# Attention with memory plus a gated feed-forward block on one core: w_v loaded first in two halves, a first layer norm in smaller tasks, and a new issue order

## The chip, the core and the metric

The kernel runs on one core of a Trainium2 chip. The core has a matrix engine (TensorE, PE in the profile; PEld is its loading of weights), a vector engine (VectorE, DVE), an engine for activation functions (ScalarE, ACT), a general engine (GpSimd, POOL) and SyncE (SP), which here only issues DMA transfers. ACT issues a few transfers of its own at the start. Engines run their own instruction streams in order and wait for each other by semaphores. The metric is device time in microseconds (us), the median of several runs.

## The reference

x is 2048 x 512 in bf16. It is normalised by rows, and both branches work on the result xn; x, A and B are added at the end.

```python
xn = _layernorm(x, axis=-1)
return x + _A_ref(xn, wq, wk, wv, wo, beta) + _B_ref(xn, w1, w2)
```

Branch A is attention in 32 heads of 16, over 4 segments of 512 rows one after the other. Within a segment it is causal softmax attention. Besides, a memory M (16 x 16 for each head) and a vector z run over the segments:

```python
pq = phi(qs)                       # phi(t) = t + 1 where t > 0, else exp(t)
a_mem = (pq @ M) / (pq . z + 1e-6)
o = g * a_mem + (1 - g) * a_dot    # g = sigmoid(beta), one for each head
M = M + phi(ks)^T @ vs;  z = z + sum(phi(ks))
```

The heads' outputs go through wo (512 x 512). Branch B is silu(xn @ w1) @ w2, with 1792 columns in between.

## The kernel before

All weights and one or two segments of activations stay in SBUF. The work is cut into some 1700 tasks, each one engine's short run of instructions, made by functions that add a task with its dependencies and buffers (`A(...)`, line 192). The tasks are issued in one fixed global order, the list `ORDER` of task numbers at line 64, which `Sched.run` (line 217) walks. On each engine the instructions stand in the order in which the list names its tasks. So an engine's order, and the buffer that a task gets from a ring, are settled when the program is built; the costs and due times in the task calls do not move anything once `ORDER` is written out. SP's DMA queue is in order as well: a transfer that waits for its data holds up every later one.

The main loop has 72 blocks of scores ("quads", line 899 and after), 18 for each segment. A block is: 4 to 12 matmuls of k (kB) and q (qT) for four head groups at a time, into psS, which takes four PSUM banks and exists once; an exp of all of it on ACT (L870, 128 x 2048 elements); and two causal masks on POOL (L889). The next block can begin when this exp has ended. Between two blocks TensorE does other matmuls, some ten of 512 columns: the projections to q, k and v, the feed-forward h (w_1) and its second product (w_2), the output projection (wo), the memory's products (M, psN), or one P times V (PV, two banks at once). These all share four other PSUM banks (`banks`), each of which must be copied out, mostly by DVE (the copies at L742, L790, L807, L958, L1178, L1203, L1228), before its next use.

Names used below: xn is a normalised tile of 128 rows (DVE, L617), xnT its transpose, stats the bn_stats of a tile (L583) with its aggregate (L584) and the addition of eps (L586), rstd the power -0.5 on POOL (L606). kB is k with every second head group masked out (L747 on POOL, for the first tile L721 and L723). V is the v projection with a column of ones; VS is V with its 64-row halves exchanged, made by two DMAs for each segment (L819). N and O are the copies of even and odd P times V; Z, Zg, Zr, dR and R are the steps by which the softmax denominators go through DRAM, are inverted, and come back repeated for every element of a head (den, Dr likewise for the memory's denominators); L1144 multiplies N by R. phiK is the transposed phi(k), made by a transposing DMA (L761).

The start, which the change touches: x's first four tiles are loaded one by one, two on SP's queue and two on ACT's; then half of w_k (its first 256 columns) on SP, half of w_q on ACT, then on SP all of w_v, w_1 in two halves with x's next four tiles between them, and the other halves of w_k and w_q. The first segment's layer norm (`ln(0)`) goes tile by tile. Tile 2 has its statistics from ACT (mean, sq), the other three from DVE, each in one task (stats, aggregate, eps). Then POOL's rstd, DVE's xn, four transposes on TensorE (L630) and one copy to xnT for each tile, on ACT for tiles 0 to 2 and on DVE for tile 3. TensorE meanwhile repeats a dummy matmul of the identity ("warm"). The first q and k tile is cut by row tiles; both, and v's first row tile, precede the first block of scores.

Of the kernel before, what the change touches and what calls it, by code (L numbers as in the profile page):

```python
# [10 lines left out]
BF16 = mybir.dt.bfloat16  # L11
# [53 lines left out]
1 3 5 14 27 0 2 53 63 28 29 15 30 31 32 64 33 54 34 4 35 36 58 55 37 38 39 40 41 42 65 59 60  # L65
43 44 45 66 70 46 71 47 56 57 48 49 50 51 67 61 62 72 52 96 109 16 6 110 68 69 97 111 7 8 9
10 98 73 74 18 114 115 99 17 116 11 112 113 100 117 19 147 101 102 184 118 103 136 129 12 130
185 131 187 148 149 132 137 150 104 105 138 188 189 268 269 270 139 76 75 271 272 13 151 133
280 106 281 282 283 140 77 284 78 84 124 273 186 192 125 107 285 126 127 193 143 81 128 274
275 82 276 277 119 120 121 122 21 123 135 196 168 278 279 169 170 108 83 171 194 172 286 287  # L70
288 289 163 164 197 142 141 190 200 79 298 299 300 301 292 80 293 290 294 85 295 291 134 86
199 201 302 87 165 89 166 167 204 152 153 154 296 297 155 328 198 329 330 202 331 205 156 179
303 203 90 180 173 332 333 88 208 209 181 191 195 182 159 144 145 304 158 305 157 160 183 220
222 221 210 212 213 306 307 161 352 353 354 355 356 214 215 358 308 309 382 383 384 385 216
217 310 311 312 386 206 313 314 363 364 146 315 428 429 430 357 431 175 226 227 211 365 366
367 432 316 317 318 319 207 218 320 22 321 371 372 373 374 230 671 219 672 673 674 223 231
375 228 176 234 177 433 225 368 235 675 229 434 224 91 435 436 420 437 174 421 390 391 178
376 392 393 237 92 238 239 322 323 324 325 326 422 394 443 444 445 236 446 377 676 423 424
241 242 243 438 439 327 440 369 447 441 20 240 359 334 335 336 337 442 338 339 677 678 246
247 401 402 403 404 405 232 340 360 341 342 343 346 347 348 349 93 450 23 233 250 679 361 244  # L80
680 344 345 350 351 94 245 409 410 411 412 413 251 248 370 262 264 254 487 252 488 406 407
489 572 162 451 452 453 454 455 456 457 458 459 460 461 462 463 464 465 466 397 255 256 253
580 490 263 467 491 258 259 257 492 362 681 493 494 517 689 690 691 692 693 495 249 496 571
587 588 398 497 498 260 499 261 579 581 682 518 519 694 500 425 501 520 399 400 582 589 387
521 583 522 523 524 388 590 591 265 266 449 469 584 448 683 592 684 685 573 686 687 525 389
595 526 527 596 267 695 696 697 24 698 502 574 426 427 585 528 529 530 531 599 688 503 594
504 593 505 597 701 702 703 704 506 408 470 471 699 700 395 577 578 507 600 602 705 508 603
872 873 874 586 601 509 875 510 511 512 532 706 604 533 416 534 598 606 535 607 536 605 513
608 514 515 623 417 475 610 611 537 476 538 516 713 25 575 576 378 472 539 624 26 540 714 715
379 380 719 716 541 477 612 615 720 396 721 717 718 625 478 722 542 543 876 544 616 545 755  # L90
756 757 479 619 758 836 837 838 546 839 483 614 723 724 759 831 731 481 613 732 609 733 734
618 620 629 832 735 833 707 474 415 840 708 736 841 842 617 621 418 853 834 835 473 709 710
843 844 482 630 711 622 633 846 712 847 848 634 468 845 849 850 626 627 637 414 638 381 812
813 814 815 743 766 744 628 635 480 767 768 769 641 485 762 486 484 553 554 555 877 816 559
556 745 560 631 878 746 561 642 562 645 640 770 557 774 636 737 775 738 776 760 739 777 747
748 740 547 643 563 548 646 879 649 564 778 632 549 550 741 742 644 817 1097 1098 647 1099
1100 650 551 565 566 567 648 1101 639 568 653 654 569 1102 95 665 419 771 761 804 805 806 667
807 781 763 881 880 764 808 725 882 779 657 658 998 666 656 1103 1104 1105 1106 1107 885 793
794 795 796 797 726 782 727 854 660 728 729 855 659 1108 652 661 662 655 1006 651 823 663 824
825 826 997 999 749 750 751 752 664 856 857 858 827 859 860 861 862 863 1013 864 865 730 785  # L100
786 787 788 866 867 753 754 798 868 869 1014 789 1127 1000 1128 870 1129 1130 1131 1017 765
1015 668 1005 913 914 1001 1002 780 669 887 772 1003 1004 915 852 1132 1007 1008 773 670 1018
1020 916 790 1011 917 888 1021 1012 1022 958 959 918 919 920 799 1024 960 921 922 923 961
1009 892 962 783 1025 800 801 1019 1133 924 925 1026 926 927 1010 1134 1135 1136 1137 963 964
1138 965 1029 1115 1116 1117 802 570 1118 1030 1109 1110 1111 1112 889 966 1113 851 1119 803
967 886 968 1114 1033 969 970 971 972 1016 1181 1023 1182 1031 1183 1196 1197 1198 894 1120
1199 1200 1034 1037 883 1188 1189 1190 1191 1032 1038 1192 1184 784 1028 1027 871 895 1185
# [1305 lines left out]
```

## Time and profile before

| what | value |
|---|---|
| median of 6 runs | 226.58 us (225.02 to 227.29) |
| the profiled execution's own time | 225.02 us |
| its span, first to last instruction | 223.3 us |
| granted TensorE clock | 1.00 |
| TensorE matmuls | 2800, busy 217.0 us |
| first and last block of scores begin | 11.38 and 200.94 us |
| DMA queues | SP 20.14 MB, ACT 0.52 MB |

The profile is one execution. Time in the text is counted from the span's start. A row such as "32.20 0.40 PE L504 MATMUL psS<-qT,kB" is an instruction, or a row of equal ones: start, length, engine, line of the kernel, operation, what it writes and reads; "[0.81 <-DVE N L958]" at its end says that its engine stood idle for 0.81 us before it, and whose end released it. All matmuls but transposes have line 504, that of a helper, so the names of their operands tell them apart: "ps<-xnT,w" is h, "ps<-w,hT" the second product of the feed-forward block, "ps<-Pt,V" and "ps<-Pt,VS" are P times V. Matmuls overlap (a matmul's length is longer than the distance to the next), so their price is read from start to start.

### The profile page before, as it was taken

How to read it: one execution, taken by the hardware profiler on the slowest of the kernel's cores; microseconds unless marked ns; L12 is line 12 of the kernel's file. 1: busy time of each engine (PE TensorE's matmuls, PEld its weight loads, DVE VectorE, ACT ScalarE, POOL GpSimd, SP SyncE). 2: the span in 40 equal slices, each digit the busy share in tenths (PEclk: the TensorE clock that was granted, in tenths of full speed). 3: DMA queues.
4: the chain of work that ended last, by engine and by line, in shares of the span. 5: the costliest groups of instructions: out<-in, count | busy, mean ns of one | idle time of the engine just before them, and what ended most of it. 6: DMA issues, size and time to landing. Idle time of an engine off the chain costs nothing.

```text
span 223.3 us, 6767 instructions
## 1 busy us (share of the span) xinstructions
PE 217.0 (97%) x2800; PEld 102.9 (46%) x2800; DVE 171.7 (77%) x307; ACT 181.4 (81%) x166; POOL 163.7 (73%) x281
## 2 busy tenths in 40 slices
PE   7999999999999999999989999999999999999994
PEld 7634353535353434444533444344454535445553
DVE  3799896778978688779995839996747696685993
ACT  4499999999899997999979787899999798995100
POOL 2748989786889878688999777848858877648420
PEclk9999999999999999999999999999999999999999
DMA  5982933490164433060136631003235200023402
GB/s 175 366 261 49 154 99 109 109 294 4 24 90 93 85 82 82 29 187 8 26 82 133 117 90 53 0 15 88 73 99 137 76 21 3 13 73 109 163 14 94
DMA packets 30851, 21.10 MB, mean 95 GB/s; under 512 B 15972, under 2 KB 29924, under 8 KB 30820
## 3 DMA queue, kind: packets, MB, share of 16 engines
q1 hardware_dynamic: 30004, 20.14, 34.9%
q10 hardware_dynamic: 816, 0.52, 0.7%
q8 instruction: 22, 0.36, 0.7%
q14 instruction: 9, 0.07, 0.1%
HBM read 11.73 MB, written 2.64 MB: 64 GB/s over the span
## 4 chain that ended last, share of the span: by engine, by line
PE 82%; DMA 6%; DVE 4%; POOL 4%; ACT 2%; issue 1%; DVEq 0%; POOLq 0%; ACTq 0%
PE ps L504 69%; PE psS L504 13%; DMA phiK<-pkT 2%; POOL Pt L889 2%; ACT Pt L870 1%; DMA R<-dR 1%; DMA x_all<-in_A_x_dram 1%; DVE xn L617 1%; DMA dR<-Zr 1%; POOL rstd L606 1%; DVE st L583 1%; POOL pkT L675 1%; ACT pkT L672 0%; POOL kB L747 0%; DVE N L958 0%
## 5 line engine op out<-in xcount | busy, mean ns | idle before, releaser
L870 ACT ACTIVATE Pt<-psS 128x2048 bf16<-128x2048 f32 x72 | 135.2, 1878 | 15.3 <-PE psS L504 10.4
L889 POOL TENSOR_SCALAR_AFFINE_SELECT Pt<-Pt 64x512 bf16<-64x512 bf16 (+1 forms) x144 | 91.0, 638 | 29.3 <-ACT Pt L870 22.5
L504 PE MATMUL ps<-xnT,w 128*128 128x512 bf16 x224 | 60.2, 380 | 0.0
L504 PE MATMUL ps<-w,hT 128*128 128x512 bf16 (+1 forms) x210 | 52.6, 366 | 0.8 <-DVE N L958 0.8
L1178 DVE SCALAR_TENSOR_TENSOR hT<-hT,ps 128x512 bf16<-128x512 bf16 x56 | 37.7, 678 | 13.9 <-ACT hT L1174 13.6
L1174 ACT ACTIVATE hT<-ps 128x512 bf16<-128x512 f32 x56 | 32.8, 597 | 1.4 <-PE ps L504 1.1
L504 PEld LDWEIGHTS <-hT 128*128 128x128 bf16 x238 | 21.5, 98 | 23.2 <-issue 3.0
L504 PEld LDWEIGHTS <-w 128*128 128x128 bf16 x224 | 20.5, 98 | 24.4 <-issue 1.9
L504 PE MATMUL psS<-qT,kB 32*128 32x256 bf16 (+5 forms) x640 | 28.6, 262 | 0.0
L747 POOL TENSOR_SCALAR kB<-kT,pm 128x512 bf16<-128x512 bf16 x30 | 22.9, 765 | 1.3
L504 PEld LDWEIGHTS <-kB 32*128 32x128 bf16 x640 | 11.6, 92 | 26.0 <-issue 23.9
L504 PE MATMUL ps<-Pt,V 64*32 64x256 bf16 (+5 forms) x640 | 20.1, 261 | 0.0
L504 PE MATMUL ps<-Pt,VS 64*32 64x256 bf16 (+5 forms) x640 | 19.0, 261 | 0.7 <-DMA VS<-V 0.5
L504 PE MATMUL ps<-xnT,w_q 128*128 128x512 bf16 (+2 forms) x72 | 18.3, 357 | 0.0
L504 PE MATMUL ps<-xnT,w_k 128*128 128x512 bf16 (+2 forms) x72 | 18.2, 357 | 0.0
L1080 POOL TENSOR_TENSOR pq<-pq,Dr 128x512 bf16<-128x512 bf16 x12 | 13.8, 1152 | 5.8 <-DMA Dr<-dE 5.6
L504 PEld LDWEIGHTS <-V 64*32 64x32 bf16 x640 | 14.1, 91 | 7.9 <-issue 2.6
L504 PE MATMUL ps<-w_v,xnT 128*128 128x512 bf16 x64 | 17.6, 380 | 0.0
L504 PE MATMUL ps<-w_o,N 128*128 128x512 bf16 (+1 forms) x57 | 15.0, 369 | 0.0
L504 PEld LDWEIGHTS <-VS 64*32 64x32 bf16 x640 | 12.9, 91 | 1.6 <-DMA VS<-V 0.8
L958 DVE CAST O<-ps 128x512 bf16<-128x512 f32 x15 | 10.3, 684 | 3.6 <-PE ps L504 3.5
L583 DVE BATCH_NORM_STATS2 st<-x_all 128x6 f32<-128x512 bf16 x15 | 10.2, 678 | 3.4 <-DMA x_all<-in_A_x_dram 3.4
(105 smaller groups left out, 254.7 us busy)
## 6 DMA issues: line engine op xcount, KB each, us to landing
w<-in_B_w_dram SPq DMA_DIRECT2D x4, 896.0 KB
VS<-V SPq DMA_DIRECT2D x8, 264.0 KB
R<-dR SPq DMA_DIRECT2D x15, 128.0 KB
out_dram<-o_t SPq DMA_DIRECT2D x15, 128.0 KB
Dr<-dE SPq DMA_DIRECT2D x12, 128.0 KB
x_all<-in_A_x_dram SPq DMA_DIRECT2D x2, 512.0 KB
N<-O SPq DMA_DIRECT2D x12, 64.0 KB
w_k<-in_A_wk_dram SPq DMA_DIRECT2D x2, 256.0 KB
```

The source lines that it names most:

```text
L504: nc.tensor.matmul(o, lhsT=l, rhs=r, start=start, stop=stop, **k)
L583: nc.vector.bn_stats(out=b.tile[:], in_=xt(t))
L606: nc.gpsimd.tensor_tensor(out=rs, in0=mv[:, t : t + n, 1:2] if first else rs, in1=lnc[:, 0:n, 1:2], op=ALU.pow,)
L617: nc.vector.tensor_scalar(out=xb.tile[:], in0=xt(t), scalar1=mv[:, t, 0:1], scalar2=rstd[:, t, 0:1], op0=ALU.subtract, op1=ALU.mult,)
L675: nc.gpsimd.tensor_scalar(out=dst_b.tile[:], in0=dst_b.tile[:], scalar1=1.0, scalar2=0.0, op0=ALU.min, op1=ALU.max,)
L747: nc.gpsimd.tensor_scalar(out=kB[u].tile[:, :, KB * r : KB * r + KB], in0=kT[u].tile[:].rearrange("p (a b) -> p a b", b=KB), scalar1=pm[:, ...
L870: nc.scalar.activation(out=pb.tile[:], in_=psS[:], func=AF.Exp, scale=SCALE)
L889: nc.gpsimd.affine_select(out=v, in_=v, compare_op=ALU.is_ge, fill=0.0, base=0, pattern=pat, channel_multiplier=-1,)
L958: nc.vector.tensor_copy(out=dst.tile[:, dt, :], in_=buf.tile[:])
L1080: nc.gpsimd.tensor_tensor(out=pb.tile[:], in0=pb.tile[:], in1=rb.tile[:], op=ALU.mult)
L1174: nc.scalar.activation(out=hb.tile[:], in_=b.tile[:], func=AF.Tanh, scale=0.5)
L1178: nc.vector.scalar_tensor_tensor(out=hb.tile[:], in0=hb.tile[:], scalar=1.0, in1=b.tile[:], op0=ALU.add, op1=ALU.mult)
```

## The change

Four edits, and a list of tasks that is new from end to end.

1. Loads. Behind x's first four tiles come now two row halves of w_v (2 of its 4 row blocks each), one on SP's and one on ACT's queue, then the half of w_k on SP and the half of w_q on ACT; the rest is as before. Users of w_v depend on both halves. The times in the calls differ too; they move nothing.
2. In `ln(0)`, statistics of tiles 1 and 3 become two tasks, bn_stats alone and the aggregate with eps, so that others may stand between them.
3. The copy of tile 0's transposes is cut in two: its first half on ACT, its second on DVE. Every user of tile 0's xnT waits for both. (`extra` is a dependency of all first users of xnT.)
4. `ORDER` is another list; it has 1724 tasks instead of 1720. All engines' streams are rearranged over the whole run. The number and shapes of instructions are the same, except for one more copy on DVE and one more DMA.

```diff
-    ld_k = [load_w(*halves(w_k, A_wk, C2, 0), "SP", 0, 5.7)]
-    ld_q = [load_w(*halves(w_q, A_wq, C2, 0), "ACTQ", 0, 6.4)]
-    ld_v = load_w(w_v[:], kv(A_wv), "SP", 0, 7.5)
+    ld_v = [
+        load_w(w_v[:, 0:2, :], kv(A_wv)[:, 0:2, :], "SP", 0, 5.2),
+        load_w(w_v[:, 2:4, :], kv(A_wv)[:, 2:4, :], "ACTQ", 0, 5.2),
+    ]
+    ld_k = [load_w(*halves(w_k, A_wk, C2, 0), "SP", 0, 6.8)]
+    ld_q = [load_w(*halves(w_q, A_wq, C2, 0), "ACTQ", 0, 6.9)]
...
+                cut = first and j in (1, 3)
...
+                if cut:
+                    st = A("DVE", 0.7, f_st, [xl[t]], due + 0.1 * j, takes=(b,), frees=(b,),
+                           label="stats")
+                    ag.append(A("DVE", 0.3, f_ag, [st], due + 0.1 * j, frees=(b,), label="aggr"))
...
+                    parts_ = (("ACT", 0, 2), ("DVE", 2, 2)) if j == 0 else (
+                        ("DVE" if j == 3 else "ACT", 0, 4),)
+                    for eng, lo, n_ in parts_:
+                        def f_e(j=j, pb=pb, eng=eng, lo=lo, n_=n_):
+                            o = xnT_b[0].tile[:, lo : lo + n_, j * P : (j + 1) * P]
...
+                        if lo:
+                            extra.append(e)
+                            e = xnT_done[s].pop()
+                        xnT_done[s].append(e)
...
-                     lambda ki: w_v[:, ki, :], (xnT_done[s] if s else [xnT_done[0][j]]) + [ld_v], label=f"v{s}{j}",
+                     lambda ki: w_v[:, ki, :], (xnT_done[s] if s else [xnT_done[0][j]] + extra) + ld_v, label=f"v{s}{j}",
```

The new order at the start, by engine. DVE: stats of tile 0 (with aggregate and eps); bn_stats of tile 1; xn of tile 0; aggregate and eps of tile 1; the two small operations for tile 2 (var); the added half copy; xn; bn_stats of tile 3, its aggregate and eps; xn; xn; the copy of v's first tile; the last copy of transposes; then q, k and masked k. TensorE: transposes, two matmuls of v, transposes, two matmuls of v, transposes, then q and k in pieces, two matmuls of the next tile's k, and the first block of scores. Between blocks of scores both orders have some ten matmuls each, of other kinds than before in most places.

## Prediction

> **What bounds the kernel now.** I read the page first, then busy time by stretch, then the chain of waits at the start, then TensorE's rows one by one.
>
> ```profile
> PE 217.0 (97%) x2800; PEld 102.9 (46%) x2800; DVE 171.7 (77%) x307; ACT 181.4 (81%) x166; POOL 163.7 (73%) x281
> PEclk9999999999999999999999999999999999999999
> ```
>
> TensorE (PE) is busy 97% of the span, at full granted clock throughout. Such a share can hide idle slots, so I cut the span at the first and last block of scores (11.38 and 200.94) and around the place where the chain leaves TensorE (111.52 to 138.00):
>
> ```profile
> 0.00:11.38 11.38, 9.71 (x97) 7.94 (x99) 6.60 (x20) 5.42 (x10) 5.34 (x27) 1.00 0.82 273
> 11.38:111.52 100.14, 100.10 (x1341) 45.03 (x1341) 82.90 (x157) 94.27 (x87) 82.22 (x143) 1.00 0.41 99
> 111.52:138.00 26.48, 24.99 (x336) 11.14 (x336) 19.38 (x35) 20.90 (x17) 23.18 (x33) 1.00 0.46 100
> 138.00:200.94 62.94, 62.94 (x838) 28.17 (x836) 47.63 (x75) 56.95 (x49) 44.51 (x70) 1.00 0.19 53
> 200.94:223.30 22.36, 19.29 (x192) 10.67 (x191) 15.17 (x24) 3.85 (x5) 8.46 (x11) 1.00 0.30 95
> ```
>
> After the length come TensorE's busy time, its weight loads, DVE, ACT, POOL. Only the third row has idle TensorE in the middle, 1.5 us. TensorE's rows give prices (timeline of TensorE):
>
> ```profile
> 32.20 0.40 PE L504 MATMUL psS<-qT,kB 32*128 32x256 bf16 x12
> 32.53 1.04 PE L504 MATMUL ps<-xnT,w 128*128 128x512 bf16 x4
> 33.41 0.59 PE L504 MATMUL ps<-xnT,w_q 128*128 128x512 bf16 x2
> 33.84 1.03 PE L504 MATMUL ps<-w_v,xnT 128*128 128x512 bf16 x4
> 34.80 0.40 PE L504 MATMUL psS<-qT,kB 32*128 32x512 bf16 x4
> ```
>
> Start to start, a matmul of 512 columns takes 0.216 us, and one block of scores with its two mode changes 0.43: 10 x 0.216 + 0.43 = 2.59 of the 2.60 seen. By the same subtraction P times V costs 1.15, a small matmul of the memory matrix 0.06, the denominator's four 0.33. With these prices nearly all of the 71 intervals between score blocks come out within 0.01 us. What is left over in all is 2.96 us: 0.40 near 86.6, 0.86 at 112.7, 0.68 at 125.6, 0.56 at 135.2, 0.46 elsewhere. So the time is: start of the first score block (11.38), a fixed amount of matmul work, 2.96 us of stalls, and a tail (22.4) that is also matmuls back to back, then the last output. Both programs have the same 2800 matmuls and 163 mode changes. The change can act through the start and the stalls alone.
>
> The start, from the chain of waits:
>
> ```profile
> 5.61 0.67 POOL rstd L606
> 6.31 0.41 DVE xn L617
> 6.72 0.61 DVE st L583
> ...
> 7.80 0.67 POOL rstd L606
> 8.51 0.42 DVE xn L617
> 8.98 0.40 PE ps L630 x4
> 9.38 2.07 PE ps L504 x13
> ```
>
> The first layer norm goes to and fro between DVE and POOL, tile after tile; no weight is in this chain after x. The three large stalls:
>
> ```profile
> 112.73 0.59 PE L504 MATMUL ps<-w,hT 128*128 128x512 bf16 x2 [0.81 <-DVE N L958]
> ...
> 125.61 0.37 PE L504 MATMUL ps<-Pt,VS 64*32 64x448 bf16 x4 [0.49 <-DMA VS<-V]
> ```
> ```profile
> 110.33 1.75 DVE L617 TENSOR_SCALAR xn<-x_all,mv,rstd 128x512 bf16<-128x512 bf16 x1 [0.36 <-POOL rstd L606]
> ```
> ```profile
> 133.32 0.67 DVE L1144 TENSOR_TENSOR N<-N,R 128x512 bf16<-128x512 bf16 x1 [3.41 <-DMA R<-dR]
> ```
>
> At 112.7 the next PSUM bank was late: its copy on DVE stood behind an xn that took 1.75 us instead of 0.41. At 125.6 the half-swapped V came late: its second transfer was issued at 121.06, with six others on SP's queue since the first. At 135.2 the copy of V stood on DVE behind a product that waited 3.41 us for R. That wait cost TensorE only 0.56.
>
> **The loads.** w_v (512 KB) leaves SP's queue as one transfer and comes back as two halves ahead of w_k and w_q, one on each queue. ACT's queue issues one more DMA (0.46, as its w_q row), so the table load, at 2.21 now, ends near 3.95; ACT's first statistic started at 4.05, so this costs nothing, with a cover of 0.1, and the var that needs it is not in the chain. When do weights land? From 2 to 7.26 us, when TensorE stopped waiting for w_k, about 1.5 MB had moved at 250 to 360 GB/s, while x, w_k and w_q halves together are 1.05 MB: up to 0.45 MB from behind had moved too. Afterwards 1.57 MB must move. So w_k and w_q land between 7.45 (strict order) and 8.7 (0.45 MB more, at 0.36 MB per us). I take 8.0, between the two. In the new order TensorE first uses w_q after the third transposes, near 8.95 (below): hidden at either end. w_v lands between 5.8 and 7.26 by the same sums; if it is the later one, the second transposes slip 0.5, off the chain.
>
> **First layer norm.** The new DVE order puts the first xn between statistics and aggregate of tile 1. rstd of tile 0 ends at 5.25 (start 4.68, 0.57), so that xn starts at 5.33 instead of 5.45. The aggregate of tile 1 follows at 5.65, its add of eps at 5.87 to 6.02 instead of 5.38 to 5.53. rstd of tile 1 starts at 6.09 instead of 5.61, and xn of tile 1 at 6.75 instead of 6.31. The added half copy of tile 0's transposes (0.42 for a whole one, so some 0.3) fits into the wait before it. Statistics of tile 3 stay behind that xn, and the whole rest moves by +0.44: next xn 8.1 (its transposes 8.55 to 8.95), last xn 8.95, last copy of transposes 9.93 instead of 9.49. DVE's copy of V (0.69), now ahead of it, ends at 9.96, beside the wait for these transposes. Then TensorE has q (0.43), k (0.43) and two k matmuls of the next tile (0.43) ahead of the first scores: 10.41 + 1.29 + 0.1 = 11.8. DVE's own copies for the first block (q 0.42, k 0.41, masked k 0.48) end near 11.5, not later. So the first scores start at 11.8 instead of 11.38. One full matmul more is done ahead of them (42 tasks against 41), worth 0.22. Net +0.2. Bounds: -0.4 if the aggregate's move costs nothing in fact and the copies go quicker; +0.8 if ACT, which now has a phi and a tanh between the first exps (exp 1.88, both 0.5 to 0.6 at their spacing), falls behind: by my sums the third block is ready 0.05 before its slot.
>
> **The order of the rest.** All SP, POOL, DVE and ACT work is reordered, so I follow the three stalls. (1) After the eighth P times V the new order has six matmuls into the one free bank before it needs the copied one: 1.3 us more than before, so 0.86 goes, unless xn takes 1.75 twice. (2) Between the two V swaps stand now xnT, Z, xnT, Z, and no longer an output and the Zg load that waits for Z: issue near 118.5, landing some 4.5 later (121.06 to 125.6 now), needed at 124.4: 0.68 goes. (3) V's copy stands ahead of the product that waits for R, and R's own transfer no longer has two phiK transposes between Zg and it: 0.56 goes. That is -2.1. Moves that I cost at nothing: w_2's second half goes behind x8 and w_o, its queue issuing it near 44; with 2.9 MB at 0.36 MB per us it lands near 52, its first use is near 58. The fourth xnT of segment 1 goes behind a phiK, ends its issue near 28.8 and lands 1.4 later (the last xnT of segment 2 ended its issue at 77.49 and k8 ran unhindered at 78.8); its user comes at 31.5. If these covers fail, TensorE waits one us for each us. What is late next: PSUM banks. I counted in both orders how much matmul work lies between the last write of a bank and its next use. A copy needs about 1.0 (0.25 until DVE starts, 0.68). Places with 1.30 or less: 11 before, 19 after. Besides the three, stalls were 0.86 in all; scaled by 19/11 that is 1.5, +0.6. The new order also has its own places of the costly kind; for their sum the rows give 0 (none) to 2.1 (a cluster like the present one). I take 1.0, as TensorE absorbed most of a 3.41 us wait. Sum of stalls: -2.1 + 0.6 + 1.0 = -0.5, bounds -1.9 (-2.96 if every stall went) and +2.
>
> A rule on (1): the 1.75 us xn lay across three POOL instructions (0.41, 0.69, 0.61 in POOL's timeline) and held up the copy until 1.16 after the block of scores; the same again would still be in time, as the bank is now needed 1.73 after it. The Trainium skill, "SBUF — State Buffer", section "Who interferes with whom", says that a DVE instruction in a two-port mode and a GpSimd instruction exclude each other for one whole instruction. By the rule the xn beside the 1.15 us POOL product that now stands there would take up to 1.6, by the row 1.75; the sum is the same by both.
>
> **Sum.** +0.2 at the start, -0.5 of stalls, 0 in the tail (same matmuls, same chain behind the last exp): -0.3 us. The profiled execution took 225.02 (span 223.3, 1.7 around it), the lowest of six; the median is 226.58. So 224.7 for its like, 226.3 for the median.
>
> **Rivals.** *B, the stalls go and nothing follows:* +0.2 - 2.1 = -1.9, 224.7. For it: the three reasons above; against it: 19 tight places. *C, slower, bank starvation:* TensorE reuses a bank whose copy on DVE, behind P times V above all, is late. Each costly site now costs 0.56 to 0.86, mean 0.70; in place of my +1.6 for new stalls stand n such sites. From +0.2 - 2.1 + 0.7 n it decides at n = 5 (+1.6, 228.2); six give 228.9. For it: 19 tight places, a DVE that is 77% busy and in order; against it: five places with 1.08 cost nothing before. *D, the start is shorter after all:* first scores at 10.9, 0.7 less with the extra matmul, and -0.5 of stalls: 225.4. It needs the chain above to be bound by weights, which no row shows. *E, the loads do nothing:* that is my forecast for them already.
>
> **How the numbers follow.** Forecast (within 1.1 us either way) 0.42; B 0.20; D 0.08; C 0.30. About 0.5% (1.1 us) is what a measurement here can tell from no change. Range: 224.5 holds B's middle, 228.6 most of C. Forecast's own range 225.4 to 227.6.
>
> **What would show it.** Right: no TensorE wait for a weight; last xn of the first norm near 8.95; first scores at 11.6 to 12.0; no waits of 0.5 at the three places; new waits of TensorE for DVE copies elsewhere, 0.3 to 0.9 each. Wrong: first scores before 11.4 or after 12.4, TensorE waiting for w_q, or stalls above 4.5 us or below 1.

## The result, and the profile after

The changed kernel takes 227.33 us (median; 225.96 to 229.79 in 32 executions), the kernel before 226.34 (224.76 to 229.63 in 69, measured beside it). The ratio is 1.0047, 95% interval 1.0029 to 1.0065: slower by 0.47%, about 1.0 us. The forecast was 0.3 us faster. The number lies inside the range that was given, but the sign is wrong, and so are several steps of the working.

The profiled execution of after took 229.3 us (span 227.4). It is one of 7 among 33 whose mean granted clock is 0.991 to 0.993 and which took 229.2 to 229.8; the other 26 took 226.0 to 228.0 at 1.00. Its trace therefore shows one loss that most executions do not have, the matmuls at half clock below.

Two lines of its page, to be held against the same two lines of before:

```profile
PE 219.0 (96%) x2800; PEld 103.8 (46%) x2800; DVE 174.9 (77%) x308; ACT 180.4 (79%) x166; POOL 160.1 (70%) x281
...
PEclk9999999999999999999999979999999999999999
```

The instructions are the same, one more on DVE (the half copy). New is the 7 in the clock. Busy time by stretch, cut as for before at the first and last block of scores, and around the place that lost most (length; busy time of TensorE, its weight loads, DVE, ACT, POOL; clock; DMA share; GB/s):

```profile
0.00:12.40 12.40, 10.41 (x98) 8.73 (x99) 6.97 (x22) 5.65 (x11) 4.33 (x24) 1.00 0.83 261
12.40:124.00 111.60, 110.65 (x1417) 49.42 (x1418) 91.27 (x171) 102.32 (x94) 89.54 (x157) 1.00 0.42 99
124.00:130.40 6.40, 4.53 (x113) 2.27 (x111) 4.12 (x7) 3.56 (x4) 3.33 (x7) 1.00 0.79 82
130.40:133.54 3.14, 3.14 (x9) 0.92 (x9) 2.46 (x3) 1.40 (x1) 3.03 (x4) 0.50 0.31 93
133.54:204.21 70.67, 70.44 (x976) 31.75 (x976) 54.76 (x84) 63.56 (x54) 51.02 (x81) 1.00 0.21 56
204.21:227.41 23.20, 19.82 (x193) 10.75 (x192) 15.28 (x24) 3.91 (x5) 8.86 (x11) 1.00 0.29 91
```

The first scores start at 12.40 instead of 11.38. In the third row TensorE is idle for 1.9 us; in the fourth, which is most of the half-clock stretch, it is busy all the time and does 9 matmuls in 3.14 us. The last stretch is 23.20 instead of 22.36. The chain of waits at the start:

```profile
2.22 7.28 DMA w_q<-in_A_wq_dram
9.49 0.05 issue
9.54 0.40 PE ps L508 x4
9.94 0.22 PE ps L648 x4
10.16 1.63 PE ps L508 x20
...
11.82 0.48 ACT kB L749
...
12.40 0.40 PE psS L508 x4
```

Before, the chain went through DVE and POOL and no weight was in it. In this execution the last link ahead of TensorE's work is w_q, and behind it stand 1.63 us of matmuls and the copy of kB. The two waits of TensorE in the middle (timeline of TensorE; the bracket is the idle time ahead of the row and what ended it):

```profile
33.09 0.59 PE L508 MATMUL ps<-xnT,w_q 128*128 128x512 bf16 x2 [0.73 <-DVE hT L1206]
...
129.40 0.40 PE L508 MATMUL psS<-qT,kB 32*128 32x256 bf16 x12 [1.87 <-ACT Pt L898]
```

What ACT and DVE did ahead of the second one (timeline of ACT, then of DVE):

```profile
122.81 1.88 ACT L898 ACTIVATE Pt<-psS 128x2048 bf16<-128x2048 f32 x1
126.95 0.63 ACT L700 ACTIVATE pkT<-kT 128x512 bf16<-128x512 bf16 x1 [2.26 <-DMA phiK<-pkT]
127.48 1.86 ACT L898 ACTIVATE Pt<-psS 128x2048 bf16<-128x2048 f32 x1
```
```profile
127.53 0.95 DVE L1145 RECIPROCAL Zf<-Zg 128x128 f32<-128x128 bf16 x1 [2.10 <-DMA Zg<-dZ]
128.40 0.63 DVE L770 CAST kT<-ps 128x512 bf16<-128x512 f32 x1
```

In the new order a phi stands ahead of the exp of block 42 on ACT, and waits 2.26 us until a transposing transfer has read its buffer; before, it stood behind that exp. On DVE the reciprocal of Zg stands ahead of a copy of kT and waits 2.10 us. Both stand in front of an instruction that TensorE needs next.

With the prices of the prediction, each interval between score blocks splits into matmul work and stall. S7 is the interval behind block 7, the blocks counted from 0. Stalls of 0.15 us and more in this trace: 0.90 at S7 (the row at 33.09), 0.37 at 63.6, 1.94 at 127 to 129, 1.55 at half clock behind it, 0.40 at 141.3; 5.16 in all against 2.52 before (a stall of 0.15 to 0.16 at S47, on the threshold, is counted in some kernels and not in others, so small differences of these sums mean nothing). None of the three old sites (112.7, 125.6, 135.2) is left.

### The profile page after: what moved, and what is told of

Its sections match the earlier page's. It is cut to its first block, busy times and chain, and to the rows that moved or that the text cites. A ratio compares the mean times of both kernels' runs of the same rounds, so it can differ in the third digit from the quotient of the medians.

```text
span 227.4 us, 6769 instructions
## 1 busy us (share of the span) xinstructions
PE 219.0 (96%) x2800; PEld 103.8 (46%) x2800; DVE 174.9 (77%) x308; ACT 180.4 (79%) x166; POOL 160.1 (70%) x281
## 4 chain that ended last, share of the span: by engine, by line
PE 71%; DMA 10%; ACT 5%; DVE 5%; POOL 4%; issue 3%; SPq 1%; ACTq 1%; POOLq 1%
PE ps L508 61%; PE psS L508 10%; ACT Pt L898 4%; DMA w_q<-in_A_wq_dram 3%; DMA phiK<-pkT 2%; DMA Dr<-dE 1%; POOL pq L1108 1%; DMA Dg<-dD 1%; DVE acc L1231 1%; DMA dD<-den 1%; DMA dE<-Dq 1%; DVE hT L1206 1%; POOL Pt L917 1%; DVE N L1172 1%; POOLq L1436 1%
## 5 line engine op out<-in xcount | busy, mean ns | idle before, releaser
L917 POOL TENSOR_SCALAR_AFFINE_SELECT Pt<-Pt 64x512 bf16<-64x512 bf16 (+1 forms) x144 | 89.9, 633 | 33.2 <-ACT Pt L898 27.9
L508 PEld LDWEIGHTS <-kB 32*128 32x128 bf16 x640 | 11.8, 92 | 28.0 <-issue 25.2
L775 POOL TENSOR_SCALAR kB<-kT,pm 128x512 bf16<-128x512 bf16 x30 | 20.6, 688 | 1.2
L508 PE MATMUL ps<-Pt,V 64*32 64x256 bf16 (+5 forms) x640 | 19.5, 260 | 0.0
L508 PE MATMUL ps<-w_v,xnT 128*128 128x512 bf16 x64 | 18.5, 396 | 0.2 <-DVE acc L1231 0.2
L986 DVE CAST N<-ps 128x512 bf16<-128x512 f32 x15 | 10.2, 682 | 5.0 <-PE ps L508 5.0
L835 DVE CAST V<-ps 128x512 bf16<-128x512 f32 x16 | 10.8, 680 | 3.0 <-PE ps L508 3.0
```

The lines of the kernel that those rows point to most:

```text
L508: nc.tensor.matmul(o, lhsT=l, rhs=r, start=start, stop=stop, **k)
L775: nc.gpsimd.tensor_scalar(out=kB[u].tile[:, :, KB * r : KB * r + KB], in0=kT[u].tile[:].rearrange("p (a b) -> p a b", b=KB), scalar1=pm[:, ...
L835: nc.vector.tensor_copy(out=bass_pair(o), in_=i)
L917: nc.gpsimd.affine_select(out=v, in_=v, compare_op=ALU.is_ge, fill=0.0, base=0, pattern=pat, channel_multiplier=-1,)
L986: nc.vector.tensor_copy(out=dst.tile[:, dt, :], in_=buf.tile[:])
```

## The experiments

Three names of theories recur in the expectations. Theories 1, 2 and 3 are the three places seen above: start, phi ahead of the exp, transposing load behind a phiK. Theory O is 2 and 3 together, "the order on the queues alone makes the waits". Theory C is not the prediction's rival C: it says that TensorE's own code, fetched over the DMA engines, holds up transfers. Theory S says that the change has a cost of its own wherever the code lies. In the table "code + 48" is a kernel whose order is untouched but whose TensorE has 48 more instructions at the very start; "+ 168" likewise.

The table gives for each kernel the ratio to before with its interval, and from its one profile the start of the first scores, the sum of stalls as above, and the time from the last scores to the end (us).

| kernel | ratio [95%] | first scores | stalls | last part |
|---|---|---|---|---|
| before | 1 | 11.38 | 2.52 | 22.37 |
| after | 1.0047 [1.0029, 1.0065] | 12.40 | 5.16 | 23.20 |
| before, new loads alone | 1.0009 [0.9967, 1.0052] | 11.97 | 2.67 | 22.49 |
| before, split layer norm alone | 0.9983 [0.9954, 1.0012] | 12.23 | 3.19 | 22.37 |
| start of after, rest of before | 0.9975 [0.9942, 1.0007] | 12.39 | 3.55 | 22.50 |
| start of before, rest of after | 0.9993 [0.9968, 1.0019] | 11.99 | 3.19 | 23.02 |
| after, phi behind the exp | 1.0027 [1.0000, 1.0054] | 12.26 | 4.53 | 22.56 |
| after, three moves | 1.0230 [1.0184, 1.0275] | 12.27 | 7.69 | 22.72 |
| before, code + 48 | 0.9950 [0.9921, 0.9979] | 12.03 | 2.41 | 22.36 |
| before, code + 104 | 0.9906 [0.9877, 0.9936] | 12.40 | 2.11 | 22.36 |
| before, code + 168 | 0.9905 [0.9872, 0.9938] | 11.49 | 1.61 | 23.24 |
| before, code + 256 | 0.9997 [0.9958, 1.0036] | 12.46 | 2.61 | 22.74 |
| after, code + 48 | 0.9976 [0.9952, 0.9999] | 12.60 | 3.33 | 22.46 |
| after, code + 104 | 0.9977 [0.9946, 1.0007] | 13.08 | 2.22 | 22.47 |
| after, code + 168 | 1.0081 [1.0047, 1.0115] | 12.87 | 3.95 | 24.07 |
| after, code + 256 | 1.0048 [1.0013, 1.0083] | 12.41 | 4.04 | 22.89 |
| + 168, new loads alone | 1.0002 [0.9968, 1.0036] | 12.38 | 1.02 | 22.95 |
| + 168, split layer norm alone | 0.9952 [0.9927, 0.9977] | 11.93 | 1.80 | 23.00 |
| + 168, start of after | 0.9988 [0.9959, 1.0018] | 13.37 | 2.95 | 23.14 |
| + 168, rest of after | 1.0012 [0.9980, 1.0045] | 14.43 | 3.23 | 23.46 |

### Taking the change apart

**New loads alone**

```diff
+    ld_v = [load_w(w_v[:, 0:2, :], ..., "SP", 0, 5.2), load_w(w_v[:, 2:4, :], ..., "ACTQ", 0, 5.2)]
     ld_k = [load_w(*halves(w_k, A_wk, C2, 0), "SP", 0, 5.7)]
     ld_q = [load_w(*halves(w_q, A_wq, C2, 0), "ACTQ", 0, 6.4)]
-    ld_v = load_w(w_v[:], kv(A_wv), "SP", 0, 7.5)
```

> The kernel before with nothing changed but the loads: w_v in two row halves right behind x, one on each queue, then w_k and w_q. Theory 1 (the late w_q costs time at the start): the first score block starts 0.6 to 1.0 us later than 11.38, TensorE waits for w_k or w_q until about 9.5, nothing changes afterwards; median 226.9 to 227.3, ratio 1.003 to 1.004. My prediction (loads hidden at either end): first scores within 0.2 of 11.38, ratio 0.999 to 1.001.

**Start of after, rest of before** (the start kernel: ORDER of after up to the first score block, then the tasks of before in their own order) **and the counterpart** (the rest kernel: start of before, rest of after).

> The changed kernel up to the first score block (new loads, first layer norm in smaller tasks), then every engine's order of before. Theory 1 (start): first scores near 12.4, one matmul more behind them, so +0.8: ratio 1.003 to 1.004. Theory 2 (what costs the time is the phi that now stands ahead of an exp on ACT in the third segment): the same start is seen, but the whole is nearer to before than to after, ratio below 1.002. Both expect the stalls of before (0.86, 0.68, 0.56) to be back and no idle of 1.9 near 129.

> The counterpart: the kernel before up to the first score block, then every engine's order of after. Theory 1 (start): first scores back at 11.4 and the time 0.8 below after, ratio 0.999 to 1.002. Theory 2 (phi ahead of the exp): idle of TensorE of 1.5 to 2 us near 128 stays, with matmuls at half rate behind it in some executions; ratio 1.004 to 1.015 as in after, and above the start kernel's. Theory 3 (the fourth xnT behind a phiK): 0.7 to 0.9 of idle near 32 stays too.

**Phi behind the exp**

```diff
-... 1185 1186 947 823 1041 1042 898 1187 ...
+... 1185 1186 947 1041 1042 823 898 1187 ...
```

> The changed kernel with one instruction moved: the phi of the third segment that waits for a transposing DMA to have read its buffer stands behind the exp of block 42 again instead of ahead of it. Theory 2: the idle of 1.9 us at 127 to 129 goes, and with it the 1.5 us of matmuls at half rate and the dip of the granted clock; time 1.5 to 3.5 below after, ratio to before 0.992 to 0.999. Theory 1 or bank starvation: the idle is replaced by another, ratio stays 1.003 to 1.006.

None of the four explains 1.0047 alone. Neither half of the change, start or rest, is measurably slower than before, and only the two together are. Moving the phi removed its stall (0.09 left at S42), but the next one came from DVE, and the time is not measurably lower than that of after. Timeline of TensorE, then of DVE, of that kernel:

```profile
129.43 0.81 PE L503 MATMUL ps<-w,hT 128*128 128x512 bf16 x3 [1.27 <-DVE kT L765]
141.34 1.02 PE L503 MATMUL ps<-w_v,xnT 128*128 128x512 bf16 x4 [1.31 <-DVE acc L1226]
```
```profile
127.88 0.95 DVE L1140 RECIPROCAL Zf<-Zg 128x128 f32<-128x128 bf16 x1 [2.23 <-DMA Zg<-dZ]
...
137.75 2.94 DVE L1167 TENSOR_TENSOR N<-N,R 128x512 bf16<-128x512 bf16 x2
```

The reciprocal waits as long as in after, and now the copy of kT behind it is what TensorE misses. The surprise is the counterpart kernel, whose queues have the same order at this place (timeline of DVE):

```profile
125.94 0.95 DVE L1113 RECIPROCAL Zf<-Zg 128x128 f32<-128x128 bf16 x1 [0.24 <-DMA Zg<-dZ]
```

Zg was issued at 123.82 there and at 123.30 in after, yet it was there 1.6 us earlier. What differs lies on the DMA engines. The DMA view of after from 124 to 126, then the same view of the counterpart (queue, packets, MB, share of the engines):

```profile
q1 hardware_dynamic: 496, 0.12, 159.9%
q8 instruction: 1, 0.02, 2.7%
```
```profile
q1 hardware_dynamic: 727, 0.25, 68.0%
```

In after one packet of 16,384 bytes of code came at 124.28, in the middle of the transposing transfer ahead of Zg: some 470 of that transfer's packets had started by 124.5, the rest started one by one until 126.0, and only then came Zg's. In the counterpart the code came at 120.5. The page of after has 22 such packets ("q8 instruction: 22, 0.36"), spread over the span some 10 us apart, and so has every other kernel here (23 where 256 instructions are added). TensorE has 5,600 instructions in the trace: 22 x 16,384 / 5,600 is 64 bytes each, 256 to a packet; the other engines have 200 to 370 each in all. One fetch lasts 0.9 to 2.0 us in these traces. If it holds one of the 16 DMA engines for so long, what that engine has to move waits. So where a fetch falls could decide which transfer is late. That is theory C, and it can be tested without touching the order.

### The position of the code

**Code + 48:** 24 of the warm-up matmuls at the start, which do no useful work, are cut in two, in both kernels.

```diff
             for _ in range(2):
-                mm(psS[:, 3, 0:P], ident[:], ident[:], True, True)
+                for c in (0, 64) if i < 12 else (0,):
+                    w_ = 64 if i < 12 else P
+                    mm(psS[:, 3, c : c + w_], ident[:], ident[:, c : c + w_], True, True)
```

> The changed kernel with its order untouched; 24 of TensorE's warm-up matmuls at the very start are cut into two halves, which adds 48 TensorE instructions and no time that counts. Theory C (the 16 KB code fetches that the trace shows on the DMA engines, one for about every 256 TensorE instructions, hold up a share of the packets of the transfer beside them): every fetch moves some 48 instructions forward, the one at 124.3 to about 120.5; the wait of the reciprocal for Zg near 127 falls from 2.1 to below 0.5 and the stalls of TensorE between 125 and 133 from 3.5 to below 1.2; time 0.5 to 2 below after. Theory O (the order on the queues alone makes these waits): the stalls stay where they are, 3 to 3.5, and the time stays at 1.003 to 1.006.

> The kernel before with the same 48 TensorE instructions added in the warm-up and nothing else. Theory C: the fetch at 122.1, which ran beside the second transfer of VS, moves to before 121 and the stall of 0.68 behind P times V goes or halves; other stalls may appear where a fetch now meets a transposing load; sum of stalls within 1.0 of 3.0, ratio 0.997 to 1.003. Theory O: all stalls as before, ratio 0.999 to 1.001.

The same with i < 26 gives + 104, with quarters for i < 14 + 168.

> The changed kernel, all warm-up matmuls cut in halves: TensorE's code shifted by 104 instructions, nothing else. Theory C (where the code fetches fall decides about 0.5 to 1% of the time in either kernel): the ratio to before lies somewhere between 0.995 and 1.008, and the stalls sit where a fetch meets a transfer that something waits for. Theory S (the change has a cost of its own besides, from its later start and its new waits, 0.2 to 0.6%): the mean over the shifts 0, 48, 104, 168 is above that of the kernel before with the same shifts by so much. If the change costs nothing of its own, the two means agree within 0.15%.

> The changed kernel, 28 warm-up matmuls cut in quarters: TensorE's code shifted by 168 instructions. Theories and numbers as for the shift by 104: ratio anywhere in 0.995 to 1.008 by theory C; with theory S the mean over the shifts is 0.2 to 0.6% above that of before.

> The kernel before, shifted by 104 TensorE instructions. Theory C: ratio anywhere in 0.994 to 1.003, the stall behind P times V near 125 between 0 and 0.9, depending on whether a fetch runs beside the second transfer of VS. If the position of the code does not matter, 0.999 to 1.001 and the same stalls as before.

> The kernel before, shifted by 168 TensorE instructions. Theory C: ratio anywhere in 0.994 to 1.003; if the position of the code does not matter, 0.999 to 1.001. Theory S: the mean of before over the shifts 0, 48, 104, 168 stays 0.2 to 0.6% below that of after.

And a whole period, 256, with quarters for i < 21 and halves for i = 21. If the cut-up warm-up itself were the cause, these two kernels would show it most.

> The kernel before, warm-up matmuls cut so that 256 TensorE instructions are added: one whole period of the code fetches. Theory C: every later fetch falls on the same instruction as in the unshifted kernel again, the fetch near 122 and the stall behind P times V near 125 are back, ratio 0.998 to 1.002. Rival (cutting the warm-up into small matmuls is what gains, through the clock or the start): ratio stays at 0.989 to 0.993 as with 104 and 168.

> The changed kernel, 256 TensorE instructions added in the same way. Theory C: fetch near 124, the reciprocal waits 2 us for Zg again, stalls of 1.3 to 3.5 between 125 and 133 are back, ratio 1.003 to 1.007 as unshifted. Rival (the cut warm-up gains): 0.996 to 0.999, as with 48 and 104.

Theory C holds: the position of the code matters, and with a period of 256 instructions. Before goes 1, 0.9950, 0.9906, 0.9905, and back to 0.9997 at 256; after goes 1.0047, 0.9976, 0.9977, 1.0081, and back to 1.0048. With a whole period added, the warm-up is cut up most of all, and the time is the old one. In the same way the two waits at 127 of after come back. The reciprocal's wait for Zg and the phi's wait for its buffer, with the time of the fetch: 2.10 and 2.26 (124.3, no shift), 0.77 and 1.88 (118.1, + 48), 0.19 and 0.72 (116.1, + 104), below 0.15 and 0.72 (115.6, + 168), and at + 256, with a fetch at 124.7 (timeline of DVE of that kernel):

```profile
127.84 0.95 DVE L1142 RECIPROCAL Zf<-Zg 128x128 f32<-128x128 bf16 x1 [2.12 <-DMA Zg<-dZ]
```

My number for + 48 was only half right: the fetch moved further forward than I wrote (118.1, not 120.5), the waits 0.77 and 1.88 were longer, and 0.76 of stall was left at S42. What stays at + 104 and + 168, 0.72 of wait and 0.40 of stall, is the order's own. The stall at S7 goes the same way: 0.90 with a fetch at 29.6 (no shift) and 1.29 with one at 30.8 (+ 256), but 0.40, nothing and 0.17 at + 48, + 104 and + 168, where no fetch falls between 29 and 31.

Packet by packet it is seen best on the second transfer of VS in before, 64 packets of 4,224 bytes. Without a fetch (shifts 48, 104, 168) all 64 run in 1.69 to 1.70 us. In before a fetch ran from 122.09 to 123.89: 60 packets had ended by 123.91, and the last four came one after another until 124.99, 1.1 us later. TensorE waited 0.49 for it at 125.61. At + 256 a fetch from 123.53 to 124.89 held up three packets by 0.67.

These places show what one fetch does to one transfer. They do not show where all of the 1% goes that before gains at + 104 and + 168: the profiled executions of before and of before + 168 differ by only 0.2 us in span (223.31 and 223.09), as the profiled execution of before was one of the quickest, and by 0.9 us in stalls. What the longer executions of before lose, no profile shows.

### Equal shifts: the change's own cost

At equal shift after is slower than before by 0.47% (0), 0.26% (48), 0.72% (104), 1.78% (168) and 0.51% (256, the same as 0). The first four average 1.0020 against 0.9940: 0.8%. Each difference is uncertain by some 0.4%, their mean by about 0.2%. After is the slower one at every position that was tried, so the change does cost something of its own, some 0.3 to 1.8%, and the 0.47% that was measured is one draw. Averages over the five profiles of each kind say where: first scores 12.67 against 11.95, stalls 3.74 against 2.25, last part 23.02 against 22.61. The spans are 225.94 against 223.65. The half clock of after's one execution is 0.3 of that.

Which part costs was tried at + 168, where before is steady.

> The kernel before shifted by 168 TensorE instructions, with the new loads alone. The shifted kernel before stands at 0.9905 with little spread. Theory S1 (the loads cost by themselves, since w_k and w_q land behind w_v): first scores about 0.6 later, ratio 0.992 to 0.995. If the loads are hidden: 0.989 to 0.991.

> The kernel before shifted by 168, with the first layer norm alone in smaller tasks. Theory S2 (the split makes the last xn 0.65 later and the first scores with it): ratio 0.992 to 0.995. If that delay is taken up by weights that land no earlier: 0.989 to 0.991.

> Shifted by 168: the start of after (loads and layer norm), every engine's order of before behind it. Theory S1 and S2 together: first scores at 12.3 to 12.9, one matmul of 0.22 more ahead of them, ratio 0.993 to 0.996. If the start costs nothing: 0.989 to 0.991, and the whole of the change's cost lies in the order of the rest.

> Shifted by 168: the start of before, every engine's order of after behind it. If the order of the rest makes the larger part of the 1.76% that after lost to before at this shift: 1.000 to 1.007. If the start makes it: 0.990 to 0.994. The two parts should add up to about 1.008 with what the start kernel shows; if they do not, they act through one another (the same DMA meeting a code fetch in one and not in the other).

From 0.9905, the start adds 0.0083 and the rest 0.0107; together 1.0095 is expected and 1.0081 was measured, so here the parts add up within the noise. Two stalls of the new order at + 168, 0.97 at 178.8 and 0.79 at 199.9, stand in the rest kernel too (0.93 and 0.56), and at no other position. Within the start the loads alone give +0.0097, the layer norm alone +0.0047 and both together +0.0083; each is uncertain by some 0.005, so their order is not shown. The loads alone have a peculiar spread: with and without the shift 6 of 12 executions ran at a mean clock of 0.992 or less and took 227.4 to 231.3, against 4 of 35 and none of 34 of before beside them (clock 0.993 or less). The two profiles of the loads alone were executions at full or nearly full clock, so where they lose it is not in a profile. The rest kernel at + 168, whose start is that of before, happened to be profiled with such a loss. Timeline of TensorE and two stretches of it:

```profile
8.74 0.40 PE L500 MATMUL ps<-xnT,w_k 128*128 128x128 bf16 x4 [1.41 <-DMA w_k<-in_A_wk_dram]
```
```profile
8.74:10.00 1.26, 1.22 (x13) 1.06 (x14) 0.23 (x1) 0.00 (x0) 1.09 (x10) 0.72 1.06 386
10.00:12.00 2.00, 1.85 (x15) 1.52 (x14) 0.89 (x3) 0.97 (x2) 0.85 (x4) 0.50 1.07 381
```

After 1.41 us of waiting for a weight the matmuls run at half rate from 9.28 to 12.70, and the first scores start at 14.43. That the loads alone lose it in the same way (they waited 0.83 and 0.93 for w_k in their profiles) is argued, not shown; in the start kernel, where w_v matmuls lie ahead of that wait, none of 12 executions had such a clock at + 168 and one of 12 without a shift. The 14.43 is of this one execution and not typical of its kernel.

### Two misses

**The split layer norm alone, no shift** (loads and order of before; on DVE the first xn stands ahead of the aggregate of tile 1, and the first transposes are copied in two halves):

> The kernel before, its loads and its order, with the first layer norm alone in smaller tasks: on DVE the first xn ahead of the aggregate of tile 1, the first transposes copied in two halves. My prediction's step (the aggregate moved, all behind it 0.44 later): last xn near 8.95 instead of 8.51 and first scores 11.6 to 11.9, ratio 1.001 to 1.003. If the start is as late as 12.3, the split alone makes the whole 0.9 of delay, and the loads nothing; if it stays at 11.4, the loads make it.

Its last xn started at 9.21, as in after (9.16), so the split alone makes that delay. The first scores at 12.23 suggest that it makes the whole delay of the scores too, but that does not follow, for w_k came late in this execution as well (timeline of TensorE):

```profile
7.47 0.40 PE L640 MATMUL ps<-ident,xn 128*128 128x128 bf16 x4 [0.66 <-DVE xn L627]
...
8.66 0.40 PE L500 MATMUL ps<-xnT,w_k 128*128 128x128 bf16 x4 [0.69 <-DMA w_k<-in_A_wk_dram]
```

In time it cost nothing that shows (0.9983).

**Three moves in after:** phi (823) behind the exp, the reciprocal and what follows it (898 to 901) behind the copies of N and O, the fourth transposing load (84) ahead of the phiK (150).

> The changed kernel with three moves: the phi of the third segment behind the exp of block 42 (ACT), the reciprocal of Zg with the three steps that follow it behind the copies of kT, N and O (DVE), the fourth transposing load of segment 1 ahead of the phiK (SP). Theory O (each of these instructions holds up a later one that TensorE needs): no stall above 0.4 at 31 and between 125 and 133, 3.5 to 4.4 less stall than in after's profile, 2 to 3 less than with the phi moved alone; ratio 0.985 to 0.995. Rival, bank starvation anywhere (what is freed here is lost at the next late bank): stalls in all stay above 4, ratio 0.999 to 1.004.

I expected 0.985 to 0.995; it is 1.023, the slowest kernel of all. The old waits are gone, and longer ones stand elsewhere. TensorE no longer waits for the transposing load; but now phiK comes behind it, and phi on ACT waits for phiK with the exp behind it (timelines of ACT and of TensorE):

```profile
32.88 0.63 ACT L695 ACTIVATE pkT<-kT 128x512 bf16<-128x512 bf16 x1 [1.86 <-DVE hT L1201]
```
```profile
35.33 0.40 PE L503 MATMUL psS<-qT,kB 32*128 32x256 bf16 x12 [1.82 <-ACT Pt L893]
...
144.48 1.02 PE L503 MATMUL ps<-w_v,xnT 128*128 128x512 bf16 x4 [2.82 <-DVE acc L1226]
```

(The row of ACT names DVE's hT. This phi waits for a DMA as well, and the phiK's last packets ended at 32.73, which fits better. Nine tenths of them had ended by 31.29; a fetch of code began at 30.97, so part of this wait is again the position of the code, and this order was run at one position only.) The later reciprocal made R later, and two products on DVE that need R took 3.57 us at 140.26, in front of the acc that frees a bank. So theory O is half true: these instructions do hold up others, but they did so at their new places too.

## Why the prediction was wrong, step by step

**Loads, "hidden at either end", "no TensorE wait for a weight": wrong.** I took w_k and w_q at 8.0, with 8.7 as the late end, and put their first use at 8.95. In after's profile the last of their packets ended at 8.67 and 8.76, and TensorE waited 0.37 for w_q until 9.54, 0.8 behind the last packet. In the four shifted profiles of after it waited 0.3 to 0.8 for w_q and 0.8 to 1.1 for w_v. I had taken the landing from one execution, and it was an early one: with the old loads TensorE used w_k from 7.27 in before's profile and 7.47 and 7.62 at + 256 and + 168, but from 8.00 (code + 48), 8.22 (+ 104), 8.66 (split layer norm alone) and 8.74 (rest kernel at + 168) in others. Still, the wait for a weight is not what makes the late start: with the phi moved, a kernel with the same start, TensorE waited for no weight in its profile, and the first scores began at 12.26.

**First layer norm, +0.44: right in kind, mis-sized.** The xn of tile 1 was to start at 6.75 and started at 6.96, the last at 8.95 and started at 9.16. The half copy did not fit into the wait; it stands between.

**First scores at 11.8: wrong, 12.40.** The term that failed is "q (0.43), k (0.43) and two k matmuls (0.43)" behind the last transposes. It took q and k of the first tiles as done by then. But the waits ahead are now filled with w_v, and both weights that the scores need come behind it; so 2.0 us of q and k matmuls (10.00 to 11.99) and a copy of kB (0.48) were left. Of the 1.02 between the two profiles, 0.22 is given back by the extra matmul. Over five pairs of profiles the difference is 0.72, because 11.38 was early for before. The step had +0.2 net; +0.5 is what these pairs give.

**Old stalls, -2.1: right at the place, one cause wrong.** All three sites are empty in after. The second VS was issued at 121.26, not near 118.5, with the scores behind it 1.8 later than in before, and still it came in time. But the 0.68 behind P times V was not "its second transfer was issued with six others on SP's queue since the first": with the same queue and shifted code it was 0.28, 0.17 and nothing, and it came back at 256 as 0.33. A code fetch made most of it. The rows of before could have told me: its DMA section has the q8 line, and a fetch stood at 122.09.

**New stalls, +1.6: wrong, 4.8 in the profile.** Of this, 1.55 is the half clock. The step "own places of the costly kind, I take 1.0" failed: it priced a cluster by the mean of the present ones, and did not look for instructions that wait for a DMA at the head of a queue. Two of those make the 1.94, most of it (all but 0.40) with the help of a code fetch, a term that the sum did not have. The 0.90 at S7 is the fourth transposing load: "lands 1.4 later" with a cover of 1.3. Its issue ended at 29.54, and TensorE's wait for four transposing loads ended at 32.9, 3.3 later; the transposing transfer ahead of it lost time to the fetch at 29.60, and without a fetch there at most 0.40 is left. The page names DVE's hT, which ended at 32.99; with code + 48 TensorE started at 32.78 while hT ran until 33.18, so it was not hT, and in the kernel with that load moved forward the wait is gone.

**Tail 0: wrong by 0.8 in the profile** (23.20 against 22.37), of which 0.22 is one more matmul behind the last scores. It varies from 22.4 to 24.1 with the position of the code; on the mean of five the difference is 0.4.

**Sum.** On the means of the five pairs of profiles the terms are +0.5 net at the start (forecast +0.2), +1.5 of stalls (forecast -0.5) and +0.2 net in the tail (forecast 0): the stalls are the term that turned the sign. Old ones went as forecast, and new ones of about twice the forecast size came, because the price of a cluster had no term for a wait on a DMA at the head of a queue, nor for a code fetch beside that DMA. Taken from the two profiles without a shift, after loses 4.3 us, while its median loses 1.0: the profile of before was the fastest of its six and the one of after one of its seven at half clock. The forecast "for its like" compared the right thing, but a difference of 0.5% can't be had from two single traces of which each has its own luck.

**Rivals.** B needed no new stalls: out. D (shorter start): out. C named the right sign, with a price (228.2 from five sites on) 0.9 too high, but another mechanism: banks late by DVE copies made 0.37 and 0.40 of after's 5.16. The loss is waits for DMA at the head of ACT's and DVE's queues, a later start, and in some executions a clock that fell.

**The rule on DVE and POOL** that was weighed at 112.7 made no difference, as foreseen: no stall is left there. The four xn of that segment took 0.40 to 1.23 us in after, so neither the 1.6 nor the 1.75 that were weighed came.

## What to carry to other kernels

Before a reordering that is worth half a per cent is credited with anything, add some dozens of idle instructions to the engine with the most code and measure again at two or three shifts: here that alone moved either kernel by 1%, and the fastest version of all is the untouched kernel before with 104 or 168 instructions more in its warm-up (0.9905 [0.9872, 0.9938] for 168). When reading a new order, list the instructions that wait for a transfer and ask what stands behind each on its engine; and ask for each transfer what happens if it lands 2 us late. A start that is read from one profile may be off by 1 us: with one and the same order of loads, TensorE had its first weight up to 1.5 us later in one profile than in another.

## What the runs showed of the hardware

**Code competes with data.** A fetch of 16 KB for each 256 TensorE instructions lasted 0.9 to 2.0 us, and about one sixteenth of the packets of a transfer beside it came that much later, as if one of the 16 DMA engines were taken: 4 of 64 packets of VS above, and in the counterpart kernel 34 of the 512 packets of the fourth transposing load, which started from 32.00 on, when a fetch of 1.51 that began at 30.50 was over. Whoever waits for the whole transfer waits for them.

**Half clock after less than 2 us.** In after TensorE was idle for 1.87 us, from 127.53 to 129.40, and 1 us later ran at 0.50, which cost 1.55. With code + 256 it was idle for 1.88 at the same place (127.86 to 129.74) and the clock stayed. The traces' record of the clock shows why. In the two traces where it fell, it changes only at points that lie 3.41 us, or a whole multiple of it, apart. In after it rises at 7.47 (matmuls of 128 columns stand 0.107 apart until then, 0.056 later), falls at 130.35, which is 36 times 3.413 later, and rises again after one more, at 133.76. (The record begins with the first rise, so the views print 1.00 ahead of it; "full granted clock throughout" does not hold for the warm-up.) In the rest kernel at + 168 it rises at 5.87, falls at 9.28 and rises at 12.70. So the half clock lasts 3.41 us both times. That fits a clock that is set anew after each stretch of 3.41 us, with the stretches lying differently in each execution (the first rise was at 4.28 to 7.47 in the 18 traces that record one). In after the whole idle time lies in one stretch; with + 256, where the clock rose at 5.82, the border at 128.70 cuts it into 0.84 and 1.04. The stretches of after, then those of code + 256 (TensorE's busy time is the first number behind the comma, the clock the last but two):

```profile
126.94:130.35 3.41, 1.54 (x79) 1.09 (x61) 2.69 (x4) 2.82 (x3) 1.61 (x3) 1.00 0.27 63
130.35:133.76 3.41, 3.41 (x16) 1.08 (x18) 2.68 (x3) 1.45 (x1) 3.25 (x5) 0.50 0.32 97
```
```profile
125.29:128.70 3.41, 2.57 (x93) 1.59 (x93) 1.29 (x2) 1.41 (x2) 0.83 (x2) 1.00 0.50 107
128.70:132.12 3.42, 2.33 (x21) 1.11 (x21) 2.56 (x5) 2.84 (x2) 2.98 (x6) 1.00 0.07 14
```

One stretch of 3.41 us at half clock makes a mean of 0.992 over the span, which is that of the 7 executions of after around 229.5. The Trainium skill, "TensorE: Matmul & The Clock Gate", section "What's actually happening", says that the half rate comes after at least one idle window of about 3.4 us, and that this window runs freely. The runs agree on the length and on the free running. They differ on the idleness, and there the measurement holds: a window with 1.87 us of idle time in after and one with a wait of 1.41 in the rest kernel were enough. Where the line lies is not shown: TensorE was busy for 1.94 of 3.41 in that window of the rest kernel, and for 1.84 in one of the start kernel at + 168 that was followed by the full clock.

**What stays open.** Why the last part varies by 1.7 us with the position of the code was not followed up. How the 0.47% without a shift divides between start and rest is not shown, since neither half alone is slower there. Whether the loads alone lose their half clock while waiting for w_k was not caught in a profile.
